# A two-stage RWKV and SwiGLU kernel: a time-slot plan replaced by one fixed order of all work, with eight shared PSUM banks and transposes by DMA

## The chip, the cores and the metric

The kernel runs on one core of a Trainium2 chip. The metric is device time in microseconds (us), from several executions of the same program. A core has these engines: PE (TensorE, matmuls; PEld is its weight load, which overlaps), DVE (VectorE), ACT (ScalarE), POOL (GpSimd) and SP (SyncE, which here only issues DMA transfers). A name with a q, such as SPq or PEq, is an engine's instruction sequencer. SBUF is the on-chip memory that holds the tiles; PSUM is the memory that PE writes its results to, used here as 8 banks of 512 float32 for each of 128 partitions. The Trainium skill, named below, is a set of notes on the chip.

A run is called slow when it is more than 1.5% above the fastest run of the same kernel.

## The reference, cut to what matters

```python
def _attn_ref(r, k, v, w, u):            # (4 batches, 8 heads, 768 steps, 48)
    state = zeros((B, H, D, D))
    for t in range(S):
        cur = einsum('bhd,bhe->bhde', u[None] * kt, vt)
        y[:, :, t] = einsum('bhd,bhde->bhe', rt, state + cur)
        state = wt[..., None] * state + einsum('bhd,bhe->bhde', kt, vt)
    return y

def _moe_ref(x, w_gate, w_val, w_out, rms_g):      # x: 3072 x 384
    xn = x / sqrt(mean(x * x, -1) + 1e-6) * rms_g
    g = xn @ w_gate                                # 384 x 1536
    return (g * sigmoid(g) * (xn @ w_val)) @ w_out # 1536 x 384
```

The output is float32, 3072 x 384. Both kernels cut the 768 steps into 6 **blocks** of 128. In a block each of the 4 batches is one **unit**. So there are 24 attention units, and 6 FFN stages of 512 tokens. Within a batch, block m+1 needs the state that block m left.

## The kernel before

An attention unit is a chain across all engines: load w, k, r, v; ln of w; prefix sums by matmul with triangular masks; exp; r and k times their decays; transposes of both; score matmuls; mask; y matmuls and a state update; a "bonus" term; a norm; a transpose of the normed x. The FFN takes four such units: 12 pairs of gate and value pieces, silu, a product, and 48 output matmuls.

Every step is a closure with a start time in a plan. The plan is sorted by time and emitted; each engine then works through its part in order.

```python
psG = tile_pool(name="psG", bufs=2, space=PSUM)   # [128, 1024] float32: sums, gate/value
psQ = tile_pool(name="psQ", bufs=2, space=PSUM)   # 512 wide: scores, output
psT = tile_pool(name="psT", bufs=2, space=PSUM)   # 512 wide: transposes, state, y
...
def cs_exp(n, j):                                 # exp of the sums goes to SBUF
    e = ewk[n, j] = pt.tile([128, 4 + 2 * DM], FP32, name="ewk", bufs=5)
    act(LN_EXP, out=e, in_=bank.pop(("cs", n, j))[:, 124:896], func=AF.Exp)
def r_mul(n, j): ...   # rA = r * e[first half], DVE
def k_mul(n, j, eng): ...   # kA = k * e[second half], DVE in blocks 0 and 1, else POOL
def tr_mm(n, j):                                  # 8 PE transposes, then two copies (ACT, DVE)
    ps = bank["tr", n, j] = psT.tile([128, 2 * NP, 128], BF16, name="ps_t")
    ...
def xn_mul(n, j):                                 # norm and rms_g in one DVE operation
    nc.vector.scalar_tensor_tensor(out=xn, in0=xb[n][:, j], scalar=rstd[n][:, 1, j:j + 1],
                                   in1=g_bc, op0=ALU.mult, op1=ALU.mult)
...
HEAD, SLOT = 4.0, 1.95
T0 = 3.0 + 8 * HEAD + 4.0
for m in range(2):                 # blocks 0 and 1: one unit every HEAD of plan time
    for j in range(SB):
        t = 3.0 + HEAD * (m * SB + j)
        at(t, ln, m, j, 1); at(t + 0.9, cs_mm, m, j); ...
at(3.0 + 5 * HEAD, load_gv, 0)     # FFN weights: cast while loading, on POOL's software queue
...
for n in range(NSB):               # FFN n fills 16 slots
    b = T0 + n * 16 * SLOT
    for f in range(FC):
        t = b + f * SLOT + 0.3
        at(t, gv_mm, n, f); at(t + 1.3, silu, n, f); at(t + 1.9, h_mul, n, f)
    ...                            # attention of block n+1 is spread over the same slots
```

## Time and profile before

The time before was 280.7 us (three runs, 280.63 to 281.16). The table gives what matters and where it was read.

| reading | value | view of the profile |
|---|---|---|
| span of the profiled run | 281.2 us | page, first line |
| PE busy | 216.8 us, 77% | page, part 1 |
| first FFN matmul | 71.0 us | timeline of PE |
| PE busy in the head | about 5 of each 10 us | windows |
| from one block's FFN start to the next | 38 us | timeline of ACT |
| PE's waits for xn after 100 us | 10.5 us | waits of PE |

First come lines of the page of the kernel before: busy time with its share of the span, PE's busy tenths in 40 equal slices, and the DMA rate in the same slices.

```profile
PE 216.8 (77%) x1668; PEld 119.1 (42%) x1688; DVE 176.9 (63%) x306; ACT 136.0 (48%) x240; POOL 115.4 (41%) x155
...
PE   1355554435899598777998878998779999999994
...
GB/s 127 200 206 216 187 216 218 206 193 185 219 188 0 0 140 3 224 197 0 0 143 211 211 0 1 59 56 2 0 0 30 85 3 0 2 84 29 2 28 84
```

Up to the tenth slice (70 us) PE is half busy while DMA moves about 200 GB/s. Later PE alternates between full slices and slices of seven or eight tenths.

These are groups of instructions of the kernel before. Each line has source line, engine, operation, output and inputs, shapes and count; then total busy us and mean ns of one; then the idle time before them and what ended it.

```profile
L235 DVE TENSOR_TENSOR qts<-ps_q,mask_lt 128x512 bf16<-128x512 f32 x48 | 31.4, 683 | 5.6 <-PE ps_q L230 5.6
...
L282 DVE SCALAR_TENSOR_TENSOR xn<-xb,rstd,g_bc 128x384 bf16<-128x384 bf16 x24 | 23.5, 978 | 10.3 <-POOL rstd L278 10.1
...
L188 POOL TENSOR_TENSOR kA<-kt,ewk 128x384 bf16<-128x384 f32 x16 | 18.7, 1171 | 24.6 <-ACT ewk L72 24.5
L184 DVE TENSOR_TENSOR rA<-rt,ewk 128x384 bf16<-128x384 f32 x24 | 18.0, 748 | 15.8 <-ACT ewk L72 10.9
...
L291 PE MATMUL ps_t<-ident,xn 128*128 128x128 bf16 x72 | 9.4, 249 | 23.9 <-DVE xn L282 23.5
```

They are DVE's mask (two for a unit), DVE's normalization, the k and r products on POOL and DVE, and PE's transposes of x, which sit behind 23.9 us of idle time.

Next is the windows view of the kernel before. The columns are the window in us, its length, busy us of PE, PEld, DVE, ACT and POOL with instruction counts, the granted PE clock, the DMA share and GB/s.

```profile
40.00:50.00 10.00, 6.09 (x60) 3.95 (x57) 7.59 (x12) 3.49 (x8) 6.93 (x11) 1.00 1.27 227
50.00:60.00 10.00, 4.74 (x46) 3.09 (x44) 6.57 (x11) 4.12 (x9) 7.20 (x10) 1.00 1.17 194
...
149.00:187.00 38.00, 32.93 (x287) 18.52 (x292) 27.85 (x51) 22.26 (x39) 19.41 (x25) 1.00 0.45 91
```

In the head no engine is full. In the last window, a block of steady work, PE is busy 33 of 38 us. The granted clock of 1.00 in the head says nothing: the trace holds no clock record before 77.6 us, and the view counts time without a record as full clock. The 384-wide matmuls of the sums take 479 to 503 ns up to 57 us, and 326 at 97 us, so PE ran slower in this head than later.

The timeline of ACT in the kernel before gives start and duration in us. The function tables that ACT loads at the switch from exp to silu mark the start of each FFN stage.

```profile
72.12 1.28 ACT L70 ACT_TABLE_LOAD   x1
...
148.58 1.28 ACT L70 ACT_TABLE_LOAD   x1
...
186.56 1.28 ACT L70 ACT_TABLE_LOAD   x1
```

These are FFN 0, 2 and 3; FFN 1 opens at 110.47 and FFN 4 at 224.00, so they are about 38 us apart. Last are PE's waits after 100 us (total, times, longest).

```profile
PE ps_t L291 <- DVE xn L282: 10.5, 9, 1.7
PE ps_g L303 <- DVE ht L311: 3.0, 4, 1.0
```

### The profile page before, as it was taken

The page shows a single profiled execution, that of the slowest core. Times are in us where ns is not written, and L with a number is a line of the kernel's source. Part 1 is how long each engine was busy: PE and PEld are TensorE (multiplying, and loading weights), DVE is VectorE, ACT ScalarE, POOL GpSimd, SP SyncE. Part 2 cuts the span into 40 slices and gives each one's busy share as a digit, 9 for nine tenths or more (in the row PEclk, how much of TensorE's full clock was granted, in tenths as well). Part 3 has the DMA queues.
Part 4 walks back from the last instruction along what each step waited for, and adds up shares of the span by engine and source line. Part 5 has one row for each costly group of instructions (what it writes and reads, how often), then busy time and mean ns, then how long its engine had stood idle before and what let it go on. Part 6 is the DMA issues. An engine that isn't in the chain of part 4 may idle for free.

```text
span 281.2 us, 4404 instructions
## 1 busy us (share of the span) xinstructions
PE 216.8 (77%) x1668; PEld 119.1 (42%) x1688; DVE 176.9 (63%) x306; ACT 136.0 (48%) x240; POOL 115.4 (41%) x155
## 2 busy tenths in 40 slices
PE   1355554435899598777998878998779999999994
PEld 0233333323343354333564334664336644554352
DVE  4477777857344235988766788648886578723430
ACT  2344443422445937335666355683447654524420
POOL 2555556592400377566272582644653301110000
PEclk9999999999999979999999999999999999999999
DMA  6999999999990060990069900110000200020002
GB/s 127 200 206 216 187 216 218 206 193 185 219 188 0 0 140 3 224 197 0 0 143 211 211 0 1 59 56 2 0 0 30 85 3 0 2 84 29 2 28 84
DMA packets 106821, 27.81 MB, mean 99 GB/s; under 512 B 99632, under 2 KB 106800, under 8 KB 106800
## 3 DMA queue, kind: packets, MB, share of 16 engines
q1 hardware_dynamic: 102528, 23.60, 42.1%
q0 software_dynamic: 3984, 3.54, 7.9%
q10 hardware_dynamic: 288, 0.39, 0.6%
q8 instruction: 13, 0.21, 0.3%
q14 instruction: 8, 0.07, 0.1%
HBM read 26.35 MB, written 4.72 MB: 110 GB/s over the span
## 4 chain that ended last, share of the span: by engine, by line
PE 34%; DVE 26%; ACT 13%; POOL 8%; SPq 8%; issue 8%; DMA 1%; ACTq 0%; POOLq 0%; DVEq 0%
PE ps_q L317 15%; PE ps_g L303 9%; SPq L92 8%; DVE qts L235 7%; DVE ht L311 6%; DVE xn L282 5%; ACT sg L72 4%; ACT L70 3%; PE ps_t L265 3%; DVE st L250 3%; DVE xb L269 2%; PE ps_t L291 2%; ACT lw L72 2%; POOL ydiag L205 2%; DVE diag L201 2%
## 5 line engine op out<-in xcount | busy, mean ns | idle before, releaser
L311 DVE TENSOR_TENSOR ht<-ps_g,sg 128x512 bf16<-128x512 f32 x72 | 49.5, 690 | 43.5 <-ACT sg L72 43.0
L72 ACT ACTIVATE sg<-ps_g 128x512 bf16<-128x512 f32 x72 | 43.1, 598 | 49.9 <-PE ps_g L303 43.2
L303 PE MATMUL ps_g<-xnt,wg_sb 128*128 128x512 bf16 x203 | 58.3, 385 | 5.1 <-DVE ht L311 3.6
L303 PE MATMUL ps_g<-xnt,wv_sb 128*128 128x512 bf16 x209 | 58.5, 386 | 0.2
L317 PE MATMUL ps_q<-wo_sb,ht 128*128 128x384 bf16 x288 | 51.5, 332 | 3.0 <-DVE ht L311 3.0
L205 POOL TENSOR_TENSOR ydiag<-vt,diag 128x384 f32<-128x384 f32 x24 | 19.9, 830 | 68.1 <-DVE diag L201 67.9
L317 PEld LDWEIGHTS <-ht 128*128 128x128 bf16 x288 | 27.9, 99 | 21.1 <-DVE ht L311 3.4
L235 DVE TENSOR_TENSOR qts<-ps_q,mask_lt 128x512 bf16<-128x512 f32 x48 | 31.4, 683 | 5.6 <-PE ps_q L230 5.6
L303 PEld LDWEIGHTS <-wv_sb 128*128 128x128 bf16 x216 | 21.4, 99 | 26.5 <-issue 1.7
L303 PEld LDWEIGHTS <-wg_sb 128*128 128x128 bf16 x216 | 20.1, 99 | 25.7 <-issue 9.7
L282 DVE SCALAR_TENSOR_TENSOR xn<-xb,rstd,g_bc 128x384 bf16<-128x384 bf16 x24 | 23.5, 978 | 10.3 <-POOL rstd L278 10.1
L294 ACT COPY xnt<-ps_t 128x384 bf16<-128x384 bf16 x24 | 11.5, 479 | 37.7 <-PE ps_t L291 37.7
L188 POOL TENSOR_TENSOR kA<-kt,ewk 128x384 bf16<-128x384 f32 x16 | 18.7, 1171 | 24.6 <-ACT ewk L72 24.5
L72 ACT ACTIVATE ewk<-ps_g 128x772 f32<-128x772 f32 x24 | 19.5, 813 | 18.6 <-PE ps_g L176 18.5
L184 DVE TENSOR_TENSOR rA<-rt,ewk 128x384 bf16<-128x384 f32 x24 | 18.0, 748 | 15.8 <-ACT ewk L72 10.9
L291 PE MATMUL ps_t<-ident,xn 128*128 128x128 bf16 x72 | 9.4, 249 | 23.9 <-DVE xn L282 23.5
L197 POOL TENSOR_TENSOR ruk<-rt,kt 128x384 f32<-128x384 f32 x24 | 24.9, 1038 | 6.8 <-DMA rt<-in_r_dram 6.8
L198 POOL TENSOR_TENSOR ruk<-ruk,u_bc 128x384 f32<-128x384 f32 x24 | 25.7, 1070 | 1.9
L273 ACT ACTIVATE junk<-xb 128x384 bf16<-128x384 bf16 x24 | 12.5, 519 | 14.1 <-DVE xb L269 14.0
L228 PE MATMUL ps_q<-rkT 48*128 48x128 bf16 x96 | 11.3, 247 | 10.2 <-DVE rkT L220 9.7
L220 DVE COPY rkT<-ps_t 128x512 bf16<-128x512 bf16 x24 | 10.1, 422 | 14.2 <-ACT rkT L217 14.0
L291 PEld LDWEIGHTS <-xn 128*128 128x128 bf16 x72 | 4.9, 106 | 32.7 <-DVE xn L282 32.1
(53 smaller groups left out, 294.7 us busy)
## 6 DMA issues: line engine op xcount, KB each, us to landing
out_dram<-ob SPq DMA_DIRECT2D x24, 192.0 KB, 1.9
wt<-in_w_dram SPq DMA_DIRECT2D x4, 768.0 KB, 6.6
kt<-in_k_dram SPq DMA_DIRECT2D x4, 768.0 KB, 7.6
rt<-in_r_dram SPq DMA_DIRECT2D x4, 768.0 KB, 10.4
vt<-in_v_dram SPq DMA_DIRECT2D x4, 768.0 KB, 9.0
wt<-in_w_dram SPq DMA_DIRECT2D x8, 192.0 KB, 3.7
kt<-in_k_dram SPq DMA_DIRECT2D x8, 192.0 KB, 3.9
rt<-in_r_dram SPq DMA_DIRECT2D x8, 192.0 KB, 3.8
```

The source lines that it names most:

```text
L72: nc.scalar.activation(**kw)
L92: nc.sync.dma_start(out=dst, in_=src(t, n, b0, nb))
L188: eng.tensor_tensor(out=kA[:, n % 2, j, :, 0:D], in0=inp[n, "k"][:, j], in1=ewk[n, j][:, 4 + DM:4 + 2 * DM].rearrange("p (h d) -> p h d", ...
L197: nc.gpsimd.tensor_tensor(out=ruk[n][:, j], in0=inp[n, "r"][:, j], in1=inp[n, "k"][:, j], op=ALU.mult)
L198: nc.gpsimd.tensor_tensor(out=ruk[n][:, j], in0=ruk[n][:, j], in1=u_bc, op=ALU.mult)
L205: nc.gpsimd.tensor_tensor(out=ydiag[n][:, j], in0=inp[n, "v"][:, j], in1=diag[n][:, j].to_broadcast([128, H, D]), op=ALU.mult)
L235: nc.vector.tensor_tensor(out=qts[n, j][:, half], in0=bank["q", n, j][half], in1=bc_mid(mask_lt, NP), op=ALU.mult)
L282: nc.vector.scalar_tensor_tensor(out=xn, in0=xb[n][:, j], scalar=rstd[n][:, 1, j:j + 1], in1=g_bc, op0=ALU.mult, op1=ALU.mult)
L291: nc.tensor.transpose(ps[:, c, :], xn[:, c * 128:(c + 1) * 128], ident)
L303: nc.tensor.matmul(ps[:, half * 512:(half + 1) * 512], lhsT=wt[:, c, f * 128:(f + 1) * 128], rhs=xnt[n][:, c, :], start=(c == 0), stop=(c ...
L311: nc.vector.tensor_tensor(out=ht[n][:, f, :], in0=bank.pop(("gv", n, f))[:, 512:1024], in1=bank.pop(("sg", n, f)), op=ALU.mult)
L317: nc.tensor.matmul(ps, lhsT=ht[n][:, f, j * L:(j + 1) * L], rhs=wo_sb[:, f, :], start=(f == 0), stop=(f == FC - 1))
```

## The change

The change replaces the plan by a fixed order of all work that a search by annealing found offline. A token names an operation, its block and unit, the slot or PSUM bank of its result (`@`) and, where there is a choice, its engine (`/`). The program executes the tokens in sequence. The table below sums up what differs; the diff after it is cut to its core.

| | before | after |
|---|---|---|
| order | start times in slots, sorted | a string of tokens, searched offline |
| PSUM | three pools, by kind of work | one tile of 8 banks, bank in the token |
| r and k products | two operations, exp in SBUF | one 768 wide, exp in place in PSUM |
| masks of a unit | two of 512 | one of 1024 |
| rms_g | in the normalization (DVE) | folded into the FFN weights (36 casts) |
| r/k and x transposes, blocks 2 to 5 | PE, then copies | 32 DMA transposes |
| FFN weights (gate, value) | cast by DMA on POOL's queue | float32 on SP's queue, in 12 pieces |
| w_out | 3 casting loads on POOL's queue | the same |
| input loads | 192 KB and 768 KB | 96 of 192 KB, in planned order |
| FFN of block 0 and 1 | after 4 units | per unit, per two units |
| PE while waiting for the first data | idle | 60 warm-up matmuls |

```diff
-psG = ...; psQ = ...; psT = ...
+self.banks = ps.tile([128, 8, 512], FP32, name="ps")
...
-def r_mul(n, j): ...
-def k_mul(n, j, eng): ...
+def cs_exp(self, m, j):
+    ps = self.b2(("cs", m, j))[:, :, 0:DM]
+    self.nc.scalar.activation(out=ps, in_=ps, func=AF.Exp)
+def rk_mul(self, m, j):
+    self.nc.vector.tensor_tensor(out=self.rkA[:, slot, :, :, 0:D], in0=self.in_rk[:, slot, j],
+        in1=self.b2(("cs", m, j))[:, :, 0:DM]..., op=ALU.mult)
...
+def tr_dma(self, m, j):
+    self.nc.sync.dma_start_transpose(out=self.rkT[:, slot], in_=self.rkA[:, slot]...)
+def xn_dma(self, m, j):
+    self.nc.sync.dma_start_transpose(out=self.xnt[:, slot, :, j * L:(j + 1) * L], in_=self.xnr[:, slot])
...
-    nc.vector.scalar_tensor_tensor(out=xn, ..., in1=g_bc, op0=ALU.mult, op1=ALU.mult)
+    self.nc.vector.tensor_scalar(out=self.xnr[:, slot], in0=self.xb[:, slot], scalar1=rstd, ...)
...
-for _, _, fn, args in sorted(plan, key=lambda e: e[:2]):
-    fn(*args)
+PLAN = """
+ld.0.0.w@0 tab.le.0 warm.0@0 warm.1 ld.0.0.v@0 warm.2 ld.0.0.k@0 warm.3 ldu warm.4 warm.5 ld.0.1.w
+...
+ldw.2.g@0 xe.0.1/V gv.0.0.0.g@6 qm.0.3@0 wc.2.h.2/A wc.1.h.1/G gv.0.1.0.g@7 ld.1.0.v@1 sq.0.2
+..."""
+for step in PLAN.split():
+    env.step(step)
```

In tokens, `ld.m.j.w` is a load of w for block m and unit j; `gv`, `si`, `hm`, `o` are the FFN's gate or value piece, silu, product and output; `cs`, `rk`, `trd`, `q`, `qm`, `y`, `st` are the attention's sums, product, DMA transpose, scores, mask, y and state; `bs` is the bonus sum, `ldo` a load of w_out, `tr` and `tre` a PE transpose with its copy (`xt`, `xe` for x).

## The prediction

> **What bounds it now.** Span 281.2 us. Two regimes. (1) The head: the timeline's first FFN matmul starts at 71.0 us. Until then the windows view gives PE about 5 of every 10 us, DVE about 7, DMA 200 GB/s: the eight units of blocks 0 and 1 run as one serial chain each, fed by 192 KB loads issued every 0.9 us, and the FFN weights wait behind the prefetch of blocks 0 to 2. Matmuls there take 0.48 us where the same shape takes 0.33 later. That fits a half clock after idleness (Trainium skill, "TensorE: Matmul & The Clock Gate", Part 1), though the granted-clock column shows 1.00. (2) The steady part: from 104.8 us blocks repeat every 37.5 us. The windows give PE 31 to 33 us busy, DVE 28, ACT 22, POOL 20. Starts in the timeline cost a block as: gate/value 12 x 1.30 us, output 4 x 1.95, four attention units of about 2.3 (sums and decay 0.43, r/k transposes 0.43, scores 0.35, state 0.34, y 0.54, x transpose 0.17): 32.6 us. The rest is waits: in the wait list PE's x transpose waits 10.5 us for DVE's xn after 100 us.
>
> **What changes.** PE: for blocks 2 to 5 the transposes go to DMA, -0.6 x 16 = -10 us; total PE work about 183 us, plus 60 warm-up matmuls while it would idle. DVE: r and k become one product reading PSUM (about 0.95 us, from 551 ns at 384 and 683 at 512 elements, against 748 plus 646 or POOL's 1171); both masks become one of about 1.2; xn loses the two-tensor form (978 ns to perhaps 0.25), as rms_g moves into the weights. About 166 us. ACT 130, POOL 94. Added: 36 weight casts of 0.3 to 0.5 us, 32 DMA transposes. Weight loads become 1 KB rows on SP, interleaved with block 0's inputs, and FFN 0 starts per unit, FFN 1 per two units, overlapping the head.
>
> **Critical path.** Splitting the new fixed order at its table loads and taking the busiest engine of each stretch (all from the durations above): to the first silu table 28 (DMA: about 18 input loads, 7 weight loads), then 20, 18, 10, 8, 12, 9, 19, 10, 22, 8, 50, and 3 us to land the last output: 217 us. That is a floor, since a stretch mixes engines in chains. I add 5%: **228 us**, range 217 to 243. Of the gain 35 to 40 us is the head, the rest removed waits and transposes. Chances: faster by over 2% 0.96, within 2% 0.02, slower 0.02.
>
> The order leaves about 4 us of other PE work between a DMA transpose and its first score matmul. The skill calls transposes as fast as ordinary copies ("Advanced Engine Details and Errata", X-Bar Transpose); no run here shows it yet.
>
> **What would show it.** First silu at 27 to 33 us; PE nearly solid (above 90%) from 50 us to the end; block period near 31 us; rk product near 0.95 us, xn near 0.25; transposes landing within 4 us and scores hardly waiting on rkT; the chain of waits mostly PE, little DVE.
>
> **What would make it wrong.** Transposes queued behind input loads on the single queue, landing at 6 us or later, so scores wait (240 us and over). Weight loads slower than 1.2 us each, which holds FFN 0. DVE not keeping up: 29 of 31 us in mid blocks.

## The result, and the profile after

The changed kernel took 226.13 us (median of four runs, 223.34 to 228.66), against 280.82 us for the kernel before in the same rounds (four runs, 280.63 to 281.16). The ratio is 0.797, with a 95% interval of 0.791 to 0.803: faster. It is computed from fast runs alone, so it is not the ratio of the medians (226.13 lies between two fast runs, 223.34 and 225.01, and two slow ones, 227.26 and 228.66). The outputs were correct, here and in all runs below.

Two of the four runs were slow, and the profiled one (227.26 us, span 225.3) is one of them. I therefore also ran the same kernel again, and its profiled run was fast (221.21 us, span 219.3). Where a reading depends on that, both are given.

Lines of the page of the kernel after (slow run), with one more: the granted PE clock in tenths.

```profile
PE 201.3 (89%) x1833; PEld 122.6 (54%) x1844; DVE 161.5 (72%) x274; ACT 121.7 (54%) x215; POOL 98.4 (44%) x142
...
PE   7698879974987999898499999799999999999993
...
PEclk9999999996799999999799999999999999999999
...
GB/s 128 188 206 257 314 281 256 196 195 172 93 165 206 203 219 229 160 212 139 168 196 181 173 217 181 192 213 158 113 54 168 162 20 52 0 70 38 1 88 87
```

PE is now mostly at seven tenths or more from the first slice on. Two slices show 4: the tenth (51 to 56 us, a hole that the experiments look at) and the twentieth (107 to 113 us). The clock is lowered in both. PE's total fell from 216.8 to 201.3 us although 16.5 us of warm-up matmuls were added. So its real work fell to 184.8 us. The transposes explain about 12 of these 32 us (experiment 5 puts them back, and PE's total is 213.5). Another 7.7 go with the warm-ups (without them PE's total is 192.5, experiment 3). I did not split the rest. Some matmul records are missing (20 of 1688 before, 11 of 1844 after), so both totals can be a little low.

Groups of the kernel after, as above.

```profile
L364 DVE TENSOR_TENSOR rkA<-in_rk,ps 128x768 bf16<-128x768 f32 x24 | 22.3, 949 | 17.6 <-ACT ps L361 10.1
L392 DVE TENSOR_TENSOR qts<-ps,mask_lt 128x1024 bf16<-128x1024 f32 x24 | 28.8, 1216 | 1.9 <-PE ps L389 1.8
...
L462 DVE TENSOR_SCALAR xnr<-xb,rstd 128x384 bf16<-128x384 bf16 x24 | 10.4, 433 | 1.9 <-POOL rstd L459 1.1 <-DMA xnt<-xnr 0.5
```

One 949 ns product replaces 748 plus 1171 ns on two engines (748 plus 646 on DVE alone in blocks 0 and 1). One 1216 ns mask replaces two of 683. The normalization fell from 978 to 433 ns.

The timeline of ACT, its table loads, in the kernel after. Those shown open FFN stages: the first work of block 0, then blocks 2, 3 and 4.

```profile
26.18 1.28 ACT L322 ACT_TABLE_LOAD   x1
...
108.92 1.28 ACT L322 ACT_TABLE_LOAD   x1
...
141.98 1.28 ACT L322 ACT_TABLE_LOAD   x1
...
171.88 1.28 ACT L322 ACT_TABLE_LOAD   x1
```

FFN work starts at 26 us instead of 72. The stage of block 2 starts at 108.9 us instead of 148.6. The periods after it are 33.1 and 29.9 us instead of 38.0 and 37.4.

The r/k tile that DMA transposes write, in the kernel after: durations on the issuing sequencer in ns (minimum, median, maximum), and the time from issue to landing.

```profile
L369 SPq DMA_TRANSPOSE rkT<-rkA x16: 1231/1282/2574, 86.1 to 175.0; - x16
...
DMA to landing us min/median/max: 3.1/3.3/4.6
```

Last, the windows view of the kernel after.

```profile
50.00:60.00 10.00, 6.57 (x47) 3.32 (x46) 1.68 (x3) 3.22 (x7) 4.77 (x5) 0.66 0.88 162
...
135.00:150.00 15.00, 13.41 (x114) 7.58 (x113) 11.63 (x23) 8.93 (x16) 12.33 (x16) 1.00 0.91 191
150.00:165.00 15.00, 14.89 (x126) 8.03 (x127) 14.01 (x22) 9.06 (x17) 9.88 (x13) 1.00 0.67 140
```

From 120 to 210 us PE is busy 13.4 to 15.0 of each 15 us. In the window from 50 us it is busy 6.6 of 10 at a clock of 0.66. By the trace's clock records the clock is 0.50 from 52.3 to 59.1 us and from 110.3 to 113.7. Both times it falls during or just after idle time of PE (50.2 to 53.6 and 108.6 to 110.0 us), but an idle stretch of 1.6 us from 66.7 us has no such record, so this is what came before it and not a rule.

**Where the time came from.** I split both traces at the silu table load of block 2, which both kernels pass with FFN 0 and 1 finished (prefetch and the first steps of the next block differ a little). The numbers come from the timeline of ACT and the spans.

| | to block 2's FFN | from there to the end | span |
|---|---|---|---|
| before | 148.6 | 132.6 | 281.2 |
| after, slow run | 108.9 | 116.4 | 225.3 |
| after, fast run | 103.1 | 116.3 | 219.3 |

Of 55.9 us (slow run), 39.7 lie before that mark and 16.2 after it. The two profiled runs of the new kernel, one slow and one fast, differ only before it. The experiments ask what earned each part, and what the run-to-run difference is.

### The profile page after: what moved, and what is told of

It reads as the page before. It is cut to its first block, busy times and chain, and to the rows that moved or that the text cites. A ratio compares the mean times of both kernels' runs of the same rounds, so it can differ in the third digit from the quotient of the medians.

```text
span 225.3 us, 4834 instructions
## 1 busy us (share of the span) xinstructions
PE 201.3 (89%) x1833; PEld 122.6 (54%) x1844; DVE 161.5 (72%) x274; ACT 121.7 (54%) x215; POOL 98.4 (44%) x142
## 4 chain that ended last, share of the span: by engine, by line
PE 48%; SPq 17%; DMA 14%; DVE 9%; POOL 5%; issue 4%; ACT 2%; DVEq 0%; POOLq 0%; ACTq 0%
PE ps L493 28%; PE ps L509 14%; SPq L288 12%; DMA in_w<-in_w_dram 5%; SPq L305 3%; DMA stage_x<-in_moe_w_gate_dram 3%; DMA xnt<-xnr 2%; DVE rkA L364 2%; DVE qts L392 2%; DMA in_rk<-in_k_dram 2%; PE ps L389 2%; DMA rkT<-rkA 2%; DVE st L423 1%; PE ps L356 1%; POOL ruk L437 1%
## 5 line engine op out<-in xcount | busy, mean ns | idle before, releaser
L497 ACT ACTIVATE sg<-ps 128x512 bf16<-128x512 f32 x72 | 42.1, 595 | 45.5 <-PE ps L493 38.1
L501 DVE TENSOR_TENSOR ht<-ps,sg 128x512 bf16<-128x512 f32 x72 | 47.8, 684 | 14.2 <-PE ps L493 7.5
L493 PE MATMUL ps<-xnt,wg 128*128 128x128 bf16 (+2 forms) x354 | 54.5, 296 | 2.0 <-DMA xnt<-xnr 0.7
L493 PE MATMUL ps<-xnt,wv 128*128 128x128 bf16 (+2 forms) x355 | 54.5, 293 | 1.3 <-ACT wv L312 0.7
L509 PE MATMUL ps<-wo,ht 128*128 128x384 bf16 x288 | 53.1, 334 | 1.1 <-DMA wo<-in_moe_w_out_dram 1.1
L493 PEld LDWEIGHTS <-wg 128*128 128x128 bf16 x360 | 28.7, 98 | 18.3 <-issue 2.9
L493 PEld LDWEIGHTS <-wv 128*128 128x128 bf16 x360 | 28.2, 98 | 17.7 <-ACT wv L312 0.9
L433 POOL TENSOR_TENSOR ruk<-in_rk 128x384 f32<-128x384 f32 x24 | 24.1, 1002 | 26.3 <-DMA in_rk<-in_r_dram 16.5
L364 DVE TENSOR_TENSOR rkA<-in_rk,ps 128x768 bf16<-128x768 f32 x24 | 22.3, 949 | 17.6 <-ACT ps L361 10.1
L392 DVE TENSOR_TENSOR qts<-ps,mask_lt 128x1024 bf16<-128x1024 f32 x24 | 28.8, 1216 | 1.9 <-PE ps L389 1.8
L480 PE MATMUL ps<-mask_lt 128*128 128x512 bf16 x60 | 16.5, 410 | 1.4 <-POOL mask_lt L253 1.4
L331 DVE COPY obr<-ps 128x384 f32<-128x384 f32 x13 | 7.1, 553 | 13.4 <-PE ps L509 13.3
L423 DVE TENSOR_TENSOR st<-ps,wcr 48x192 bf16<-48x192 f32 x40 | 13.6, 351 | 3.8 <-PE ps L416 3.4
```

Of the source, the lines that this page charges most:

```text
L364: self.nc.vector.tensor_tensor(out=self.rkA[:, self.slot["rkA", m, j], :, :, 0:D], in0=self.in_rk[:, self.slot["in_rk", m], j], in1=self.b ...
L392: self.nc.vector.tensor_tensor(out=self.qts[:, self.slot["qts", m, j]].rearrange("p a q t -> p (a q) t"), in0=self.b2(("qb", m, j)).rearra ...
L433: self.nc.gpsimd.tensor_tensor(out=self.ruk[:, self.slot["ruk", m, j]], in0=rk[:, 0], in1=rk[:, 1], op=ALU.mult)
L480: self.nc.tensor.matmul(self.b1(("warmb",)), lhsT=self.mask_lt, rhs=bc_mid(self.mask_lt, 4), start=True, stop=True)
L493: self.nc.tensor.matmul(ps[:, a * n:(a + 1) * n], lhsT=w[:, c, f * 128:(f + 1) * 128], rhs=x[:, c], start=(a == 0 and c == 0), stop=(a == ...
L497: self.nc.scalar.activation(out=self.sg[:, self.slot["sg", m, g, i]], in_=self.b1(("gvb", m, g, i, "g")), func=AF.Silu)
```

## The experiments

My theory was that the head's gain comes from order (FFN 0 and 1 overlap with loads and attention), and that the rest comes from cheaper operations and from transposes taken off PE. The rivals were: that the order alone, and not the operations, gives the second part; that the warm-up matmuls earn the head; and that DMA transposes are a side issue. Experiments 4 and 7 came from a flaw that the first run showed. Each run was beside runs of the kernel before on the same chip (medians there: 282.16, 282.06 and 282.61 us in the three groups: 1 to 4, 5 to 8, 9 to 10).

### 1. The same kernel again

The edit: none.

> The changed kernel once more, unedited, for its spread (223.3 to 228.7 us in four runs against 0.2% for the kernel before) and for a second trace. Both theories: 223 to 229 us, ratio 0.795 to 0.81. If the spread comes from the wait near 46 to 54 us, where block 1's decay input lands late, the second trace shows another length of that wait; if it is spread over the whole run, that wait is the same length.

Measured: 221.21, 225.08, 229.60 and 229.74 us; the last three count as slow. The median, 227.34, is within the first result's range. Dividing both traces by the table loads, one stretch differs most, the third: from 46.36 to 71.17 us in the slow run, 24.8 us long, against 20.6 in the fast one. I had estimated 18.

The timeline of ACT in this stretch of the slow run (the bracket is the idle time before the instruction and what ended it):

```profile
46.36 1.28 ACT L322 ACT_TABLE_LOAD   x1
52.65 1.76 ACT L325 ACTIVATE lw<-in_w 128x384 bf16<-128x384 f32 x4 [5.00 <-DMA in_w<-in_w_dram]
```

ACT sits idle for 5.0 us because block 1's w has not landed. The chain of waits in this window (start, duration in us):

```profile
41.68 10.94 DMA in_w<-in_w_dram
...
52.65 0.94 ACT lw L325 x2
...
53.64 0.80 PE ps L356 x2
```

The load was issued at 41.68 and took 10.94 us; the median of such a load over the whole run is 4.0 us. In the fast run the wait for w is 2.2 us, and the chain goes through another load instead:

```profile
41.17 11.17 DMA in_rk<-in_r_dram
...
52.40 1.00 POOL ruk L433
```

So in both runs loads issued at 41 us are slow: block 1's last w takes 10.9 us in the slow run and 8.5 in the fast one, the next r loads 11.0 to 11.6 in both. In the slow run PE stands idle for 3.4 us (50.2 to 53.6), and then works at the lowered clock until 59.1; in the fast run no idle time of PE in this stretch lasts as long as 1 us before 61 us, and the clock stays at 1.00. PE is busy for 5.4 us at half clock there. If half of that is lost, it is 2.7 us (an estimate), more than half of the 4.2 us between the two stretches.

What delays them is visible in the trace's DMA packets, which I counted by queue in steps of 2 us (q0 is POOL's software queue, q1 is SP's; rate in GB/s as written, mean duration of a packet in ns):

```
slow run        q0 GB/s, ns      q1 GB/s, ns
40 to 42 us       0               197,  18
42 to 44 us      18, 129          148,  16
44 to 46 us     157,  83           20,  21
46 to 48 us     126,  77           72,  20
48 to 50 us     131,  75           51,  23
50 to 52 us     146,  77           41,  25
```

The three w_out loads on POOL's queue run from 42 us on, with packets four times as long as those of SP's 192-byte rows. While they run, SP's queue falls from 197 to between 20 and 72 GB/s. The Trainium skill, "DMA: Bandwidth & Descriptors", section "Queues, rings and completion order", states that each DMA engine takes turns between its queues packet by packet. If they alternate one for one, with a packet of the trace as one turn, SP's share of time is 16 / (16 + 77) = 17%, and 17% of its 197 GB/s is 34 GB/s, an estimate from the trace's own packet times. The measured 20 to 72 is around that, and from 44 to 52 us the trace has 1497 packets of q0 and 1950 of q1, not far from one for one. The order between POOL's issues and SP's last w and r loads, a few us apart, is not fixed, which fits the run-to-run difference. Which of several factors tips it in a given run I have not shown.

### 2. PE transposes put back into the new order

The edit, for all of blocks 2 to 5 (`trd` to `tr`, `tre`; `xd` to `xt`, `xe`), each in a bank that was free there, with the copy directly after:

```diff
-... rk.2.1@3 trd.2.0@2 st.2.0@1 ...
+... rk.2.1@3 st.2.0@1 tr.2.0@2 tre.2.0@2/A ...
```

> The changed kernel with all 32 DMA transposes done by TensorE again (8+3 transposes a unit and one PSUM copy each, alternating ACT and DVE, in banks that are free there). Theory A (PE paces the run from 60 us on, so the 16 x 0.6 = 9.8 us of PE work come on top): 233 to 238 us. Rival B (the single DMA queue, about 90% busy to 150 us, and the 3.3 us landing of a transpose pace the middle; giving the queue 32 transfers less pays for the PE work): 223 to 229 us.

Measured: 249.9 us (247.39 to 255.48), ratio 0.883 (0.878 to 0.888). Neither theory's range held it; it was slower. The waits of PE in its profiled run (255.48 us, a slow one) point to the cause (total us, times, longest):

```profile
PE ps L493 <- DVE rkT L331: 4.7, 6, 0.8
PE ps L493 <- ACT rkT L335: 3.5, 4, 1.1
```

L493 is an FFN matmul. With two smaller waits for copies of x transposes (1.7 and 1.1) it waits 11.0 us for copies; those now hold PSUM banks that FFN pieces were meant to take. The experiment measured my placement as much as the transposes, so I repeated it.

### 3. No warm-up matmuls

The edit: the 60 `warm` tokens are removed.

> The changed kernel without its 60 warm-up matmuls (13 us of PE at full clock) in the head. Theory A (the head is paced by DMA, which is at 100% from 2 to 56 us, so a colder PE costs nothing): within 2 us of the unedited kernel. Rival B (three units' matmuls at half clock lengthen the chain to the first gate matmul): first silu later by 2 us or more, and 3 to 6 us more in all.

Measured: 223.37 us (222.16 to 223.60), ratio 0.791 (0.788 to 0.794). Nothing clear is lost. All four runs were fast. The groups of PE in the first 15 us show that the warm-ups do work on durations. First the kernel after, then the one without warm-ups:

```profile
L377 PE MATMUL ps<-ident,rkA 128*128 128x128 bf16 x16 | 1.2, 220 | 0.0
...
L356 PE MATMUL ps<-lw,mask_lt 128*128 128x384 bf16 x2 | 0.6, 324 | 1.8 <-ACT lw L325 1.8
```

```profile
L370 PE MATMUL ps<-ident,rkA 128*128 128x128 bf16 x16 | 2.1, 309 | 1.4 <-POOL ruk L426 1.4
...
L349 PE MATMUL ps<-lw,mask_lt 128*128 128x384 bf16 x2 | 1.0, 479 | 8.2 <-ACT lw L318 8.2
```

A transpose takes 220 ns after warm-ups and 309 without, and a 384-wide matmul 324 instead of 479. That agrees with the Trainium skill, "TensorE: Matmul & The Clock Gate", Part 1, where the array starts at half clock and needs sustained work to leave it; the granted-clock column of the profile is 1.00 in both. That column misleads: the first clock record stands at 4.5 us in the kernel after and at 30.7 us without warm-ups, and time before it counts as full clock. But the first silu table load comes at 26.77 us instead of 26.18 (25.12 in the fast run of the unedited kernel), less than the rival's 2 us later, so PE's speed is not what paces the head. The rival that warm-ups earn the head falls.

### 4. w before k in the loads of block 1, unit 2

The edit swaps two tokens so that the last w load is issued before the w_out loads:

```diff
-... gv.0.3.1.g@7 ld.1.2.k wc.5.h.2/G ... ldo.0 ld.1.2.w gv.0.1.2.v@0
+... gv.0.3.1.g@7 ld.1.2.w wc.5.h.2/G ... ldo.0 ld.1.2.k gv.0.1.2.v@0
```

> The changed kernel with one swap in the order of loads: the decay input of unit 2 of block 1, which the first cumulative sums wait for at 52.6 us, goes before its k, so that it is issued ahead of the output-weight loads on the other queue. Theory A (while those weight loads run, their 768-byte packets leave the 192-byte input packets about 40 of 207 GB/s; what is issued before them lands in time): the sums start 3 us or more earlier, total 2 to 5 us less. Rival B (the bytes have to come in any order, the wait only moves to k and r): within 1.5 us.

Measured: 223.22 us (221.92 to 224.82), ratio 0.792 (0.787 to 0.797), all four runs fast. The w loads now land within 5.0 us, and the k load that changed places with one takes 7.7 instead of 3.8, which supports the reading that the w_out loads slow what is issued beside them. The sums of block 1 start at 49.3 instead of 53.6 us in the slow run; in the fast run of the unedited kernel they start at 49.7. By the ratios the total is 1.4 us less (0.005 of 282), with overlapping intervals, so theory A's 2 to 5 us are not shown and rival B's range holds it. The wait moved: all waits in 38 to 60 us are now led by this line.

```profile
POOL ruk L430 <- DMA in_rk<-in_r_dram: 6.0, 1, 6.0
```

The r load of the same unit now lands last, after 12.3 us, and the bonus sum behind POOL's product stands first in DVE's order and holds what follows.

### 5. PE transposes put back, with better places

As in 2, but each transpose takes the bank whose next user is farthest away, and its copy comes one PE piece later.

```diff
-... trd.2.0@2 st.2.0@1 dke.2@0 cs.2.2@2 cs.2.3@6 sn1.2.0 ...
+... st.2.0@1 dke.2@0 cs.2.2@2 tr.2.0@5 cs.2.3@6 tre.2.0@2/A sn1.2.0 ...
```

> TensorE transposes once more in the changed kernel, but placed with care: each takes the bank whose next user in the fixed order is farthest away, and its copy stands one TensorE piece later instead of directly behind the transpose. The first try cost 24 us where the added TensorE work is 9.8 us; its wait list has FFN matmuls waiting about 10 us for the copies, which share their banks. Theory A (most of the excess was the bank reuse that the edit made): 233 to 240 us. Rival B (the fixed order has no room for 64 more instructions wherever they stand): 245 us or more.

Measured: 239.12 us (236.50 to 242.52), ratio 0.845 (0.839 to 0.852). In its profiled run (242.52 us, a slow one) the FFN matmul's longest wait is no longer for a copy of a transpose:

```profile
PE ps L493 <- ACT wv L312: 1.2, 1, 1.2
```

By the ratios, which compare fast runs, this is 13.6 us more (0.048 of 282 us); experiment 2 was 24.3 more. The start times in the trace before price the PE work at 0.6 us a unit, 9.6 us for 16 units, but PE's busy total rose by 12.2 us (201.3 to 213.5), so most of the cost is the PE work itself. DMA transposes are worth about 14 us in this order. It may be an upper bound: the order was searched for DMA transposes, and my placement was not searched.

### 6. The kernel before with DMA transposes

The edit in the kernel before. r and k products share a tile, so that one DMA transposes both. The loads of blocks 4 and 5 are cut into 192 KB pieces, so that no transpose waits long behind one on the shared queue.

```diff
-    rA = persist.tile([128, 2, SB, H, PD], BF16)
-    kA = persist.tile([128, 2, SB, H, PD], BF16)
+    rkA = persist.tile([128, 2, SB, 2, H, PD], BF16)
+    rA, kA = rkA[:, :, :, 0], rkA[:, :, :, 1]
...
-            at(t, tr_mm, m, j)
-            at(t + 0.6, tr_r, m, j)
-            at(t + 0.6, tr_k, m, j)
+            at(t, tr_dma, m, j)
...
-            at(t + 0.8, xn_mm, m, j)
-            at(t + 1.4, xn_out, m, j)
+            at(t + 0.8, xn_dma, m, j)
```

> The kernel before with one part of the change alone: blocks 2 to 5 transpose r, k and x by DMA from one merged r/k tile; the loads of blocks 4 and 5 are cut to 192 KB pieces and spread so that the transposes on the same queue are not stuck behind 768 KB. Theory A (its block period of 37.5 us is waits of a time-slot order around about 33 us of PE work, so 2.4 us less PE work and a longer latency move it little): 275 to 284 us. Rival B (PE paces each block, all of it shows): 268 to 273 us.

Measured: 273.74 us (272.28 to 276.14), ratio 0.972 (0.966 to 0.978). That is 8.3 us less than the kernel before, where the start times put the PE time removed at 9.6 us and PE's busy total fell by 11.9 (216.8 to 204.9); it lies between the ranges and partly in both, so neither theory is chosen. PE still waits in the old order (whole run):

```profile
PE ps_g L311 <- DVE ht L319: 15.0, 14, 2.0
PE ps_t L299 <- DVE xn L290: 13.0, 8, 3.7
```

So in the old order DMA transposes alone give 8 of the 55 us.

### 7. w first, and the bonus sum later

Experiment 4 plus one more token: the bonus sum of unit 2 moves behind the mask of unit 1, so that DVE does not stand at the late r load.

```diff
-... tr.1.1@0 bs.1.2 ld.1.2.v ... qm.1.1@1 ld.2.0.k ...
+... tr.1.1@0 ld.1.2.v ... qm.1.1@1 bs.1.2 ld.2.0.k ...
```

> The changed kernel with the w and k loads of unit 2 of block 1 swapped, and the DVE row sum of that unit's bonus moved 12 steps later, behind the products and masks of units 0 and 1. In the swap alone the w wait went away but POOL waited 6 us for that unit's r and DVE waited 3.6 us for POOL's product, in front of work that was ready. Theory A: that DVE wait goes, stretch from the second to the third table switch 20 us instead of 23, total 219 to 222 us. Rival B (the bytes pace the head whatever the order): 222 to 225 us as with the swap alone.

Measured: 221.56 us (220.89 to 221.99), ratio 0.787 (0.783 to 0.790). The four runs lie within 0.5% and are all fast. The window over the former hole:

```profile
50.00:60.00 10.00, 9.63 (x113) 6.45 (x110) 6.36 (x10) 4.56 (x8) 4.68 (x5) 1.00 1.06 211
```

PE is busy 9.63 of 10 us from 50 us on, at full clock, where the kernel after had 6.57 at 0.66 in the slow run and 9.20 at 1.00 in the fast one. The third stretch took 19.2 us, and the whole span is 218.9. Experiment 4 still had a stretch of half clock there (57.7 to 61.1 us, after PE stood idle from 55.3 to 57.4); here there is none. Its interval lies just below that of the first result (0.791 to 0.803), which came from other rounds and rests on two fast runs: 1.3% less. The fastest run of the unedited kernel, 221.21 us, lies within this version's range, so a gain over its best runs is not shown. The eight runs of the unedited kernel spread from 221.21 to 229.74 us; that the edit removes this spread is likely but not shown, since experiment 3, which keeps the old load order, also spread little in its four runs.

### 8. The same without warm-ups

The edit: experiment 7, and the 60 `warm` tokens removed.

> As the run before it, and without the 60 warm-up matmuls, which cost or gained nothing clear alone (222.2 to 223.6 us). Theory A (the warm-ups do nothing, head paced by DMA): the same within 1.5 us as the run before it, and a small spread. Rival B (they bring the first gate matmul forward by about 1 us, and that is kept): 1 to 2 us slower than the run before it.

Measured: 222.72 us (221.66 to 223.90), ratio 0.790 (0.786 to 0.795). This is about 1 us above experiment 7, with overlapping intervals, so whether warm-ups help by that much stays open.

### 9. The new operations in the old order

The edit keeps all operations of the kernel after and puts the tokens in the order of the old plan's start times, with whole-block FFN stages. To be free of deadlocks and races it needs larger rings, fewer weight stages, and the w loads of blocks 0 and 1 first.

```diff
- 'rkA': 6, ... 'ruk': 2, ... 'xb': 4, ... 'ydr': 5
+ 'rkA': 8, ... 'ruk': 4, ... 'xb': 8, ... 'ydr': 8
-NSTAGE, NWG, NOQ = 7, 6, 3
-GROUPS = {0: ((0, 1), (1, 1), (2, 1), (3, 1)), 1: ((0, 2), (2, 2)), 2: ((0, 4),), ...}
+NSTAGE, NWG, NOQ = 4, 6, 3
+GROUPS = {m: ((0, 4),) for m in range(6)}
-PLAN = """ld.0.0.w@0 tab.le.0 warm.0@0 ..."""
+PLAN = """tab.le.0 ldu ld.0.0.w@0 ld.0.1.w ld.0.2.w ld.0.3.w ld.0.0.k@0 ..."""   # sorted by the old times
```

> All operations of the changed kernel (one r/k product, one mask, scaled weights without the second tensor in xn, DMA transposes, single PSUM tile) emitted in the time-slot order of the kernel before: blocks 0 and 1 through attention first, FFN 0 after them, one fixed slot of 1.95 us per FFN piece; no warm-ups; loads of blocks 2 to 5 as that order has them, weights cast as they come. Theory A (the order is most of the gain; cheaper operations off the path change little beyond the 8 us that the DMA transposes gave alone): 255 to 272 us. Rival B (the cheaper operations are most of the gain, the order only polishes): 230 to 245 us.

Measured: 268.10 us (266.13 to 268.61), ratio 0.948 (0.943 to 0.953). The split at the silu table load of block 2 is what I wanted from it.

| | to block 2's FFN | from there to the end |
|---|---|---|
| before | 148.6 | 132.6 |
| before with DMA transposes (6) | 142.0 | 128.4 |
| new operations, old order (9) | 151.0 | 115.5 |
| after (slow run) | 108.9 | 116.4 |
| w first, late sum (7) | 104.0 | 114.9 |

The second column answers for the later part. The new operations in the old order reach 115.5 us, as good as the annealed order with 116.4. There the operations earn the gain (4.2 of the 17.1 us with the DMA transposes alone, by the row of experiment 6), and the order adds nothing that shows. Block periods in this run are 32.7, 31.4 and 31.3 us by the timeline.

The first column needs one more cut, at the first silu table load. From there to block 2's the old order takes 67.9 us with the new operations (83.1 to 151.0) and 76.5 with the old ones (72.1 to 148.6). So the operations save 8.6 us there too. The time to the first silu they did not shorten: it is 83 us instead of 72. That must be read with care, since it is an artifact of my edit. PE's waits up to 100 us are led by

```profile
PE ps L377 <- ACT rkT L323: 25.1, 4, 11.2
```

which is ACT, in fixed order, standing at weight casts whose data has not landed (ACT's own waits: 9.7 us for a value piece, 8.3 for a gate piece). What the run does show is that operations alone, in the old order, give 8.6 + 17.1 = 25.7 us after the first silu. The rest of 55.9 us, about 30, I put down to the order by subtraction; what the operations do before the first silu stays open. By whole times the bounds are wider: the operations in the old order saved 14.5 us (282.61 to 268.10, artifact included), and the new order of the same operations then took off about 42 more (268.10 to 226.13; that step also brings back the warm-ups and the smaller rings).

### 10. FFN 0 held back until block 0 is complete

The edit moves the 16 earliest FFN 0 tokens of units 0 to 2 behind the last x transpose of block 0 (`xe.0.3`), and leaves all else in place.

```diff
-ldw.2.g@0 xe.0.1/V gv.0.0.0.g@6 qm.0.3@0 wc.2.h.2/A wc.1.h.1/G gv.0.1.0.g@7 ld.1.0.v@1 ...
+ldw.2.g@0 xe.0.1/V qm.0.3@0 wc.2.h.2/A wc.1.h.1/G ld.1.0.v@1 ...
+... xe.0.3/A gv.0.0.0.g@0 sn.0.3 gv.0.1.0.g@7 ld.1.1.v si.0.0.0@0 ...
```

> The changed kernel with block 0's FFN held until all four units of block 0 are through (16 steps that stood before the last transposed x of block 0 moved behind it, one to every other step). Theory A (the head to 57 us is paced by DMA, so a later start of 6 us of TensorE work falls where TensorE waits anyway): 0 to 4 us more than the unedited kernel. Rival B (the early start per unit is what shortens the head): 6 to 10 us more.

Measured: 228.96 us (227.14 to 229.84), ratio 0.809 (0.804 to 0.815), against 0.797 for the kernel after in other rounds: about 1.5% or 3.4 us more. Rival B's 6 to 10 us fall. The trace shows where it goes: PE stands idle from 27.6 to 31.4 and from 32.5 to 35.7 us, the clock is 0.50 from 28.8 to 39.1, and the second stretch takes 26.5 us instead of 20.2; but the third then takes 17.7 us instead of 24.8 (slow run) or 20.6 (fast run). So starting FFN 0 before its block is complete is worth about 3 us by these runs, and since slow runs of the unedited kernel took 225.1 to 229.7 us, even that is not sure. That the rest of the head's gain comes from FFN weights early among the loads, and from FFN 0 and 1 as work that fills waits of attention, is my reading and not shown. I did not split it further, and how much each of these gives stays open.

## Why the prediction was right

The prediction was 228 us (217 to 243); 226.13 was measured. Its steps, one by one:

- **"to the first silu table 28":** it came at 26.2 us (25.1 in the fast run). Right.
- **The stretch sum of 217 us as a floor:** the stretches as predicted and measured (slow run; fast run; the first counts from the table load at 0.72 us) were 28 (25.5; 24.4), 20 (20.2; 20.1), 18 (24.8; 20.6), 10 (9.0; 9.0), 8 (8.2; 8.2), 12 (11.0; 10.7), 9 (9.6; 9.4), 19 (21.9; 23.4), 10 (11.2; 9.7), 22 (22.2; 21.4), 8 (7.7; 8.2) and 53 (53.4; 53.4). In the slow run eleven of twelve are within 3 us, and the third is 6.8 above. In the fast run the third is 2.6 above and the eighth 4.4. Four of the slow run's stretches came in below their number, so the floor holds for the sum only. The eighth holds the second lowered clock (0.89 in 105 to 120 us of the slow run, 0.80 in the fast one). In the fast run it lasts from 104.1 to 110.9 us and begins at the end of an idle time of PE (102.7 to 104.2); what lowers it I did not test. Experiment 7 reached a span of 218.9 with three tokens moved, so the sum was close to what this order can do.
- **"I add 5%":** 11 us. Right in size for the slow run (8.3), too much for the fast ones (2.3). I had put it down to stretches that mix engines in chains. In the slow run most of it was one place, where loads on one queue starve beside another's and PE then runs at the lowered clock. So the closeness of 228 to 226.13 is in part luck: the allowance was meant for something else, and the median lies between fast and slow runs.
- **"Of the gain 35 to 40 us is the head, the rest removed waits and transposes":** 39.7 and 16.2 us in the slow run, 45.5 and 16.3 in the fast one. Right in place, and too small for the fast run's head. Experiment 9 adds that 8.6 us of the head's part come from the cheaper operations in FFN 0 and 1, and that the operations alone, in the old order, gain as much in the second part.
- **"rk product near 0.95 us":** 949 ns. **Masks "of about 1.2":** 1216 ns. Right.
- **"xn ... near 0.25":** 433 ns on average, 319 in the median and up to 1045. Wrong in size, by 0.18 us for each of 24. Of the 24, 15 took 302 to 320 ns. Seven of the other nine began while a two-tensor product of POOL's was running and ended 116 to 120 ns after that product did (the one of 1045 ns after a product that ran 929 ns into it), and the last two overlap a weight cast of POOL's. So the trace has DVE standing until POOL is done there. PE's waits for DVE's xn are nearly gone all the same.
- **"Transposes landing within 4 us and scores hardly waiting on rkT":** 3.3 us in the median, 4.6 at most, and PE's scores wait 1.4 us in total. Nearly right. The Trainium skill's "Advanced Engine Details and Errata", section "X-Bar Transpose (TRN2)", calls transposes as fast as regular DMAs. Here a transpose of 256 KB lands in 3.3 us and an input load of 192 KB in 3.7 to 4.1 us, so the trace agrees.
- **"PE nearly solid (above 90%) from 50 us to the end":** from 120 to 210 us it is 89% to nearly 100%, and from 70 to 100 us 93% or more in both runs; from 50 to 60 us it was 66% in the slow run and 92% in the fast one, from 60 to 70 us 79% in both, and from 100 to 110 us 70% in both. Partly right. The step that failed is the third stretch, for which I took the busiest engine's time and left out what w_out on POOL's queue does to the loads on SP's, and the lowered clock after the hole: 24.8 us (slow run) or 20.6 (fast run) instead of 18.
- **"block period near 31 us":** 33.1 and 29.9, mean 31.5. Right.
- **"total PE work about 183 us":** 184.8 without warm-ups. Right. **"plus 60 warm-up matmuls while it would idle":** they cost nothing, and they gain nothing that shows (experiments 3 and 8).
- **What would make it wrong:** transposes landing at 6 us or later did not come. The other two came near without holding anything that shows: a weight load's packets fill the 16 DMA engines for 1.25 us (by their durations), and DVE is busy 27.1 of 29.9 us in the period from 142 us, where PE is busy 28.6. The one trouble that did come, the starved loads, was not on the list.

## What to carry to other kernels

When a new order and new operations come in one change, replay the new operations in the old order, and split the times at a mark that both kernels pass: here the operations earned about 26 of 56 us after the first silu, and the order, by subtraction, about 30. A load on one queue can be slowed by long packets on another (here from 4 to 11 us), so issue what is needed next ahead of a bulk load on any queue, and then check what now stands first at each waiting engine; three moved tokens took the hole out of the trace here, and with it the lowered clock after it. With PSUM banks assigned by a plan, the place of an operation put in by hand can cost as much as its work (24.3 us with a careless bank and 13.6 with a better one, where PE's busy total rose by 12.2).

## What the Trainium skill lacked or had wrong

- "DMA: Bandwidth & Descriptors", "Queues, rings and completion order", states the turn-taking by packet but not what follows for unequal packets: here the queue with 192-byte rows fell from 197 GB/s to between 20 and 72 beside casting loads whose packets took about 77 ns against 16 to 25, and a 192 KB load took 11 us instead of 4.
- No page that I used says how to read a profile before its first clock record. Here it comes at 4.5 us with warm-ups, at 30.7 without, and at 77.6 in the kernel before. The granted-clock column shows 1.00 before it all the same, while a 384-wide matmul takes 478 ns and more before it and 322 to 327 after it, outside the stretches of lowered clock. The durations have to be read instead.
- I found bandwidths of DMA transposes in the skill, but no time from issue to landing of one between two SBUF tiles on this chip: here 128 x 1024 bf16 landed 3.3 us after issue (3.1 to 4.6), and 128 x 384 bf16 2.5 us (2.3 to 4.2).
